# Packed attention, a mixture of experts and a soft mixture on one core: w1's loads on another queue, combine steps and a second attention group at other slots

## The chip, the core and the metric

The kernel runs on one core of a Trainium2 chip. Its engines work side by side, each through a queue of its own, strictly in order: TensorE (PE, with its weight loads PEld), VectorE (DVE), ScalarE (ACT), GpSimd (POOL) and SyncE (SP, which here only issues DMAs). The metric is the device time of one execution in microseconds, the median of a few runs.

## What is computed

```
p_packed = softmax(p k^T / 8) v          # 4 batches, 8 heads, 576 tokens, 32 packed tokens, d 64
x = softmax(q p_packed^T / 8) p_packed   # as rows: 2304 x 512
x = sum_e prob[:, e] * (relu(x @ w1[e]) @ w2[e])                  # 4 experts, F = 1024
logits = x @ phi                                                  # 32 slots
d = softmax over rows;  slots = d^T x;  per slot's expert: relu(slots @ m1) @ m2     # 8 experts
out = softmax over slots(logits) @ slot_out
```

All of it in float32. The big products are split: `a`, the second attention matrix, and `g`, the packed tokens times w1, are each held as a rounded part and a residue in float32r, and three of the four products are taken.

## The kernel before

Attention is not multiplied out. For each batch, p_packed (tile `pkn`) is multiplied with w1 first, and the result `g` then with the attention matrix `a`: that is the relu's input h. The logits come from h through `wphi`, w2 times phi, which the kernel makes once at the start.

**Slots.** The main loop runs over 128 slots, 32 a batch. A slot is one 128-wide piece of F: 12 matmuls give two banks h (L620), ScalarE takes relu (L630) and GpSimd multiplies by the expert's probability (L631); every second slot, VectorE does both for one of the banks (L625). One slot later VectorE transposes the piece into `hr` (L641, `flip_h`). Each fourth slot also makes the next `g` (`make_g`: 16 matmuls L585, two casts on ScalarE L595, two residues on VectorE L597), then loads the next half expert of w1 (`load_w1`, tile `w`, 1 MB) into its single buffer, and adds the last four pieces to the logits (`logits`, L653).

**What is hung onto slots.** A table `todo` and generators put other work behind a slot's matmuls:
- `attention` for the next batch, as two groups of heads (g = 0, 1) of 18 stages, one a slot, begun at the slots `ATT_AT` of the batch. The stages that matter here: 0 transposes of k (`kt`, L344, then q's load); 2 scores `sa` on PE; 3 row maxima (L382); 4 exponentials `ex` on ScalarE (L395); 5 normalisation on VectorE (L408 to L413); 6 transposition `et` on PE (L419); 7 copies of et and transposes of q; 8 `pv` on PE, 9 copies into `pkn` by ScalarE and VectorE (L468, L471); 10 scores `sb` on PE; 11 `nat` on VectorE (L500, L506; it frees sb's banks); 12 to 15 subtract, exponential, sum ("add", L520 to L522), multiply, by turns on GpSimd, ScalarE, VectorE, GpSimd; 16 transposition; 17 `hi`, ScalarE's cast to `a` (L537), and `lo`, its residue (L542).
- `softmaxes` of the batch before, over rows for d and over slots for the combine. The steps to d and the pooling (`POOL_AT`, L775) come first; the remaining six are the combine steps at `C_AT`: den and the row minimum on VectorE (L740, L743; from the second batch on also L735, L738), subtract on GpSimd (L745), exponential on ScalarE (L749), sum on VectorE (L751 to L753), multiply on GpSimd (L755), transposition into `cts` on VectorE (L758).
- w2's way to wphi (`wphi_ops`), for eight pieces n in the first slots: four rounds of w2t on PE and a copy back by ScalarE (L260, L267), `pw` (L275), ScalarE's copy of it (`pick`, L286), `wp` (`back`, L291), ScalarE's copy of that (`keep`, L294). Two ScalarE operations of it are let out per slot.

PE's results go through eight PSUM banks of which six rotate, the one idle longest first (`mm_ps`). A DMA that is issued waits, besides for its buffer, for the earlier DMA that uses the same one of eight completion semaphores.

**The order** of the program is written by hand (`manual_schedule`), except that the work of the head, before slot 0, is placed by `place_ops` with costs; what it leaves over (rank 2) runs in the slots in the order of its list. All loads go through SP's queue, dprobs' excepted.

**The tail**, after slot 127, streams 42 MB of w2, m1 and m2 in 512 KB chunks through whatever buffers are free, and computes the slots' experts and the output from it. The stream begins in the last batch.

Of the kernel before, what the change touches and what calls it, by code (L numbers as in the profile page):

```python
# [9 lines left out]
F32 = mybir.dt.float32  # L10
F32R = mybir.dt.float32r
AF = mybir.ActivationFunctionType
ALU = mybir.AluOpType
# [5 lines left out]
def tile_packed_attention_moe_softmoe(  # L19
# [21 lines left out]
    NB, H, S, D = q.shape  # L41
# [7 lines left out]
    NCH = NE * DF // FC  # L49
# [7 lines left out]
    HT_BUFS = 5  # L57
    W2_BUFS = 4
    POOL_AT = (5, 6, 7)
    ATT_AT = (8, 12)  # L60
    C_AT = (8, 9, 10, 11, 12, 13)
    SPREAD_AT = (2, 3)
    RING = NE + 1

# [103 lines left out]
    def load_w1(t=None):  # L168
        n = w1_n[0]
        if n >= NB * NCH:  # L170
            return
        w1_n[0] += 1
        e, hf = order[n // 2], n % 2
        if t is None:
            t = w1_pool.tile([128, NDC, FC], F32, tag="w1", name=f"w1_{n}")
        sp.dma_start(
            t, w1[e, :, FC * hf : FC * hf + FC].rearrange("(c p) f -> p c f", p=128)
        )
        w1_t[n] = t
# [18 lines left out]


    class Op:  # L200
        def __init__(self, stage, eng, cost, fn, deps, take=0, give=0, rank=0):
            self.stage, self.eng, self.cost, self.fn = stage, eng, cost, fn
            self.deps, self.take, self.give, self.rank = list(deps), take, give, rank
            self.end = None
# [41 lines left out]
        )  # L246
        w2_t[n] = t

    def wphi_ops(n, loaded, next_load):

        st = {}
        ops = []
# [1 line left out]
        def turn(x):  # L254
            t = st.setdefault("t", None)
            if t is None:
                t = st["t"] = w2_t.pop(n)
            st[x] = mm_ps(f"w2t{n}_{x}", keep=True)
            for dc in range(NDC):
                pe.transpose(  # L260
                    st[x][:, 128 * dc : 128 * dc + 128],
                    t[:, x, 128 * dc : 128 * dc + 128],
                    ident,
                )

        def put(x):
            act.copy(st["t"][:, x, :], st[x])  # L267
            let_go([st[x]])
# [24 lines left out]
        def keep():  # L293
# [2 lines left out]
            )  # L296
            let_go([st["ps"]])

        puts = []
        for x in range(4):  # L300
            ops.append(Op(0, "PE", 0.47, lambda x=x: turn(x), [loaded], take=1, rank=2))
            ops.append(Op(0, "ACT", 0.58, lambda x=x: put(x), [ops[-1]], give=1, rank=2))
            puts.append(ops[-1])
        ops.append(Op(0, "PE", 1.3, project, puts, take=1, rank=2))
        if next_load:
            next_load.deps.append(ops[-1])
            ops.append(next_load)
        pr = [o for o in ops if o.fn is project]
        ops.append(Op(0, "ACT", 0.27, pick, pr, give=1, rank=2))
        ops.append(Op(0, "PE", 0.15, back, ops[-1:], take=1, rank=2))  # L310
        ops.append(Op(0, "ACT", 0.27, keep, ops[-1:], give=1, rank=2))
        return ops


# [11 lines left out]
    def attention(b, g, tmp, late, gp, loads=None):  # L326
# [212 lines left out]
        @op(17, "DVE", 0.76, hi)  # L539
        def lo():  # L540
            hl = a2_t[b, g]
            (dve if loads else gp).tensor_tensor(out=hl[1], in0=st["a2"], in1=hl[0].bitcast(F32), op=ALU.subtract)  # L542

        return ops

# [336 lines left out]
    with tc.manual_schedule():  # L882
# [89 lines left out]
        for n in range(NCH):  # L972
            after = None
            if n + W2_BUFS < NCH:
                m = n + W2_BUFS
                after = Op(
                    0, "SP", 2.5, lambda m=m: load_w2(m, w2s[m % W2_BUFS]), [], rank=2
                )
                landed.append(after)
            ops += wphi_ops(n, landed[n], after)  # L980
            ops.append(Op(0, "NONE", 0.0, done, ops[-1:], rank=2))
        rest = place_ops(ops)
        for o in list(rest):
            if o.eng == "ACT" and all(d.end is not None for d in o.deps):
                o.fn()
# [328 lines left out]
```

## Time and profile before

| | |
|---|---|
| median of 3 runs | 508.59 us (506.87 to 512.04) |
| the profiled execution | 507.49 us, its span 505.7 us |
| PE busy | 472.3 us, 93% of the span |
| DVE, POOL, ACT busy | 290.9, 204.4, 181.7 us |
| granted TensorE clock, mean | 0.976 |
| moved by DMA | 104.36 MB |

Span is from the first instruction's start to the last one's end. PE's share of busy time says little about one place; what PE waits for, and for how long, is read from the list of waits and from the order of time. In the rows, "<-X" behind idle time names what ended it. Idle time of PEld that PE does not share costs nothing.

### The profile page before, as it was taken

To read this page: it belongs to the slowest core of one execution; us is meant where nothing else is said; L and a number is where in the kernel's file an instruction comes from. 1 tells how busy PE (TensorE), PEld (TensorE's weight loads), DVE (VectorE), ACT (ScalarE), POOL (GpSimd) and SP (SyncE) were. 2 spreads that over 40 slices of the span, in tenths; PEclk is the share of its full clock that TensorE was granted. 3 is DMA by queue.
4 is the path that set the end of the run, shared out by engine and by line. 5 is a ranking of instruction groups with operands and counts; after the bars stand their busy time and mean duration, and the time that the engine had idled before them with its cause. 6 is when DMAs were issued, how large, how long until landed. Compare 5 with 4: busy or idle time off the path is not lost.

```text
span 505.7 us, 13249 instructions
## 1 busy us (share of the span) xinstructions
PE 472.3 (93%) x5608; PEld 334.9 (66%) x5608; DVE 290.9 (58%) x551; ACT 181.7 (36%) x449; POOL 204.4 (40%) x266
## 2 busy tenths in 40 slices
PE   6899799999999989999998999999999998998695
PEld 3767677778775767778566678775787866322153
DVE  3683355687781777886559588781875545100022
ACT  2475455435440434354224335440434310200033
POOL 3024233357942544586326157941656513100000
PEclk9999999999999999999999899999999997899986
DMA  8989832457231447643215243285672479999997
GB/s 197 382 311 272 298 130 81 135 136 232 84 123 47 131 141 178 177 143 112 86 68 194 71 128 103 86 294 207 244 256 85 166 275 403 414 412 412 383 383 273
DMA packets 57740, 104.36 MB, mean 206 GB/s; under 512 B 5904, under 2 KB 24848, under 8 KB 57680
## 3 DMA queue, kind: packets, MB, share of 16 engines
q1 hardware_dynamic: 57552, 103.36, 59.6%
q8 instruction: 44, 0.72, 0.6%
q0 software_dynamic: 128, 0.15, 0.3%
q14 instruction: 16, 0.13, 0.1%
HBM read 98.78 MB, written 4.72 MB: 205 GB/s over the span
## 4 chain that ended last, share of the span: by engine, by line
PE 77%; DMA 12%; DVE 6%; SPq 3%; ACT 1%; issue 1%; ACTq 0%; DVEq 0%
PE h L620 39%; PE pb L775 8%; PE lg L653 7%; PE g L585 6%; DMA ck<-in_moe_w_dram 4%; DMA hr<-in_moe_w_dram 4%; DMA w<-in_moe_w_dram 4%; PE pv L455 3%; PE sa L358 2%; PE o L1273 2%; SPq L849 2%; PE w2t L260 2%; PE sb L358 2%; PE et L419 1%; PE tt L1133 1%; PE so L1242 1%
## 5 line engine op out<-in xcount | busy, mean ns | idle before, releaser
L631 POOL TENSOR_TENSOR ht<-ht,pe 128x288 f32<-128x288 f32 x192 | 153.1, 807 | 180.0 <-ACT ht L630 179.8
L620 PEld LDWEIGHTS h<-a,g 128*128 128x128 f32 x1536 | 207.2, 188 | 23.2 <-issue 14.7
L620 PE MATMUL h<-a,g 128*128 128x288 f32 x1536 | 222.1, 300 | 0.0
L630 ACT ACTIVATE ht<-h 128x288 f32<-128x288 f32 x192 | 79.0, 412 | 173.6 <-PE h L620 166.3
L641 DVE STREAM_TRANSPOSE hr<-ht 128x576 f32<-128x576 f32 x128 | 97.3, 763 | 45.3 <-POOL ht L631 41.9
L597 DVE TENSOR_TENSOR g<-g,g 128x512 fp32r<-128x512 f32 x64 | 40.9, 679 | 26.2 <-ACT g L595 26.2
L625 DVE SCALAR_TENSOR_TENSOR ht<-h,pe 128x288 f32<-128x288 f32 x64 | 28.0, 438 | 37.5 <-PE h L620 37.5
L595 ACT CAST g<-g 128x512 fp32r<-128x512 f32 x64 | 34.5, 589 | 27.4 <-PE g L585 27.4
L775 PE MATMUL pb<-hr,d 32*32 32x512 f32 x1152 | 40.5, 598 | 0.0
L585 PE MATMUL g<-w,pkn 64*32 64x512 f32 x512 | 36.1, 601 | 2.9 <-DMA w<-in_moe_w_dram 2.8
L653 PE MATMUL lg<-ht,wphi 128*32 128x288 f32 x512 | 38.3, 412 | 0.0
L653 PEld LDWEIGHTS lg<-ht,wphi 128*32 128x32 f32 x512 | 13.5, 109 | 33.2 <-POOL ht L631 22.5
L775 PEld LDWEIGHTS pb<-hr,d 32*32 32x32 f32 x1152 | 18.3, 103 | 14.7 <-issue 10.2
L1233 DVE COPY ob<-o 128x256 f32<-128x256 f32 x12 | 4.7, 422 | 36.5 <-PE o L1273 36.2
L1242 PE MATMUL so<-hr,hm 128*32 128x256 f32 (+1 forms) x136 | 18.0, 455 | 4.7 <-DMA hr<-in_moe_w_dram 4.7
L267 ACT COPY hr<-w2t 128x512 f32<-128x512 f32 x32 | 17.5, 595 | 5.5 <-PE w2t L260 5.4
L260 PE MATMUL w2t<-ident,hr 128*128 128x128 f32 x128 | 18.3, 290 | 0.7 <-ACT pt L286 0.6
L260 PEld LDWEIGHTS w2t<-ident,hr 128*128 128x128 f32 x128 | 15.5, 149 | 3.4 <-issue 0.9
L673 POOL COPY ps<-dpn 128x576 f32<-128x576 f32 x16 | 10.6, 665 | 13.7 <-DVE dpn L195 13.7
L789 DVE SCALAR_TENSOR_TENSOR tacc<-tacc,rsc,pb 128x512 f32<-128x512 f32 x12 | 8.2, 743 | 13.2 <-PE pb L775 13.2
L1242 PEld LDWEIGHTS so<-hr,hm 128*32 128x32 f32 x136 | 6.1, 116 | 14.1 <-DMA hr<-in_moe_w_dram 9.4
L1242 PE MATMUL so<-ck,hm 128*32 128x512 f32 (+1 forms) x52 | 12.3, 531 | 1.1 <-DMA ck<-in_moe_w_dram 1.1
(159 smaller groups left out, 435.4 us busy)
## 6 DMA issues: line engine op xcount, KB each, us to landing
w<-in_moe_w_dram SPq DMA_DIRECT2D x32, 1024.0 KB, 5.2
hr<-in_moe_w_dram SPq DMA_DIRECT2D x40, 512.0 KB, 8.7
ck<-in_moe_w_dram SPq DMA_DIRECT2D x38, 512.0 KB, 8.0
hr<-in_moe_w_dram SPq DMA_DIRECT2D x8, 1024.0 KB, 10.1
k<-in_k_dram SPq DMA_DIRECT2D x16, 288.0 KB, 3.9
v<-in_v_dram SPq DMA_DIRECT2D x18, 192.0 KB, 7.0
q<-in_q_dram SPq DMA_DIRECT2D x12, 288.0 KB, 2.9
out_dram<-ob SPq DMA_DIRECT2D x8, 384.0 KB, 6.0
```

The source lines that it names most:

```text
L260: pe.transpose(st[x][:, 128 * dc : 128 * dc + 128], t[:, x, 128 * dc : 128 * dc + 128], ident,)
L585: pe.matmul(ps[g][c : c + 32, :], pkn_t[b][o : o + 64, g, hp, 0, :], t[o : o + 64, 2 * g + hp, :], start=True, stop=True, tile_position=(o ...
L595: act.copy(gg[:, 0, g], ps[g])
L597: dve.tensor_tensor(out=gg[:, 1, g], in0=ps[g], in1=gg[:, 0, g].bitcast(F32), op=ALU.subtract)
L620: pe.matmul(ps[:, :HS], gg[:, l, g, fs], m[:, ts], start=(g == 0 and i == 0), stop=(g == 1 and i == 2),)
L625: dve.scalar_tensor_tensor(out=ht[:, ts], in0=ps[:, :HS], scalar=0.0, in1=pr[:, ts], op0=ALU.max, op1=ALU.mult,)
L630: act.activation(out=ht[:, ts], in_=ps[:, :HS], func=AF.Relu)
L631: pool.tensor_tensor(out=ht[:, ts], in0=ht[:, ts], in1=pr[:, ts], op=ALU.mult)
L641: dve.transpose(out=hr[:, place(b, i), :, f0 : f0 + 32], in_=ht_t[s].rearrange("p (x t) -> p x t", t=32),)
L653: pe.matmul(lg_t[b][r][32 * x : 32 * x + 32, :HS], wphi[:, NFT * e + 4 * hf + x, :], ht_t[4 * ci + x][:, HS * r : HS * r + HS], start=(ch ...
L775: pe.matmul(pb[c][m : m + 32, :], d[o, x + par, :], hr[o, lo : hi + 1 : hi - lo, x + par, :], start=(x == 0), stop=(x == NBLK - 2), tile_p ...
L1242: pe.matmul(so[32 * e : 32 * e + 32, d0 : d0 + dw], hm[s][:, x + xl, e, :], cks[e][:, dw * xl : dw * xl + dw], start=(s == 0 and x + xl == 0),
```

## The change

Five edits. w1's loads for n = 1 to 25 are issued by ScalarE, behind the two casts of make_g; n = 0 and those of the last batch stay with SP. The six combine steps move from slots 8 to 13 of a batch to slots 17 to 26. The second attention group begins at slot 13 of a batch in place of 12. The list of w2's way back is sorted by a key, so that `wp` and its copy of piece n come behind the second w2t of piece n + 1. The residue of `a` is always VectorE's.

```
-    ATT_AT = (8, 12)
-    C_AT = (8, 9, 10, 11, 12, 13)
+    ATT_AT = (8, 13)
+    C_AT = (17, 18, 19, 21, 22, 26)
...
-        sp.dma_start(
+
+        (act if 0 < n < (NB - 1) * NCH + 2 else sp).dma_start(
             t, w1[e, :, FC * hf : FC * hf + FC].rearrange("(c p) f -> p c f", p=128)
         )
...
+        def add(eng, cost, fn, deps, key, **kw):
+            ops.append(Op(0, eng, cost, fn, deps, rank=2, key=n + key, **kw))
+            return ops[-1]
+
         puts = []
         for x in range(4):
...
+            tr = add("PE", 0.47, lambda x=x: turn(x), [loaded], 0.1 * x, take=1)
+            puts.append(add("ACT", 0.58, lambda x=x: put(x), [tr], 0.1 * x, give=1))
+        pr = add("PE", 1.3, project, puts, 0.5, take=1)
         if next_load:
-            next_load.deps.append(ops[-1])
+            next_load.deps.append(pr)
+            next_load.key = n + 0.5
             ops.append(next_load)
...
+        pk = add("ACT", 0.27, pick, [pr], 0.5, give=1)
+
+        bk = add("PE", 0.15, back, [pk], 1.15, take=1)
+        kp = add("ACT", 0.27, keep, [bk], 1.15, give=1)
+        add("NONE", 0.0, done, [kp], 1.15)
         return ops
...
-            (dve if loads else gp).tensor_tensor(out=hl[1], in0=st["a2"], in1=hl[0].bitcast(F32), op=ALU.subtract)
+            dve.tensor_tensor(out=hl[1], in0=st["a2"], in1=hl[0].bitcast(F32), op=ALU.subtract)
...
-        rest = place_ops(ops)
+        rest = sorted(place_ops(ops), key=lambda o: o.key)
```

Three places in the order, before and after. Line numbers after are two to seven higher than before (L260 is L262, L408 is L415, L641 is L648).

TensorE in the first batch, around one pw; before:

```order
L275 MATMUL pw_786<-hr,tacc 32x128 x16
L291 MATMUL wp_805<-ident,pt_803 128x128
L620 MATMUL h_0_810<-a_00_509,g_603 128x288 x3
L620 MATMUL h_0_810<-a_01_541,g_603 128x288 x3
L620 MATMUL h_1_819<-a_00_509,g_603 128x288 x3
L620 MATMUL h_1_819<-a_01_541,g_603 128x288 x3
L260 MATMUL w2t_0_827<-ident,hr 128x128 x4
L260 MATMUL w2t_1_833<-ident,hr 128x128 x4
```

The same place after:

```order
L277 MATMUL pw_786<-hr,tacc 32x128 x16
L262 MATMUL w2t_0_805<-ident,hr 128x128 x4
L627 MATMUL h_0_813<-a_00_509,g_603 128x288 x3
L627 MATMUL h_0_813<-a_01_541,g_603 128x288 x3
L627 MATMUL h_1_822<-a_00_509,g_603 128x288 x3
L627 MATMUL h_1_822<-a_01_541,g_603 128x288 x3
L262 MATMUL w2t_1_830<-ident,hr 128x128 x4
L293 MATMUL wp_836<-ident,pt_803 128x128
```

The reader of pt, wp, has moved behind the next slot and both w2t; the number of rows is the same.

VectorE at slots 12 and 13 of the second batch (g residues, then what stands ahead of the first group's normalisation, the rows of ss and ex); before:

```order
L597 TENSOR_TENSOR g_2441<-g_0_2442,g_2441 128x512
L597 TENSOR_TENSOR g_2441<-g_1_2443,g_2441 128x512
L344 STREAM_TRANSPOSE kt_2471<-k_1494 128x576
L344 STREAM_TRANSPOSE kt_2473<-k_1496 128x576
L641 STREAM_TRANSPOSE hr<-ht_2422 128x18x32
L625 SCALAR_TENSOR_TENSOR ht_2480<-h_1_2490,pe_2013 128x288
L758 STREAM_TRANSPOSE cts<-lt_1991 32x576
L408 TENSOR_SCALAR ss_2468<-ss_2468 128x1
L412 RECIPROCAL ss_2468<-ss_2468 128x1
L413 TENSOR_SCALAR ex_2467<-ex_2467,ss_2468 128x576
```

The same place after:

```order
L604 TENSOR_TENSOR g_2433<-g_0_2434,g_2433 128x512
L604 TENSOR_TENSOR g_2433<-g_1_2435,g_2433 128x512
L648 STREAM_TRANSPOSE hr<-ht_2414 128x18x32
L632 SCALAR_TENSOR_TENSOR ht_2463<-h_1_2473,pe_2013 128x288
L415 TENSOR_SCALAR ss_2459<-ss_2459 128x1
L419 RECIPROCAL ss_2459<-ss_2459 128x1
L420 TENSOR_SCALAR ex_2458<-ex_2458,ss_2459 128x576
L351 STREAM_TRANSPOSE kt_2484<-k_1540 128x576
L351 STREAM_TRANSPOSE kt_2486<-k_1542 128x576
```

The second group's k transposes have moved behind the normalisation, and the transposition into cts has gone from here. The combine's sum (L751 to L753), which stood a slot ahead of these rows, has gone too.

VectorE ahead of the second group's copy into pkn, with the next transposition behind it, slots 20 and 21 of the second batch; before:

```order
L641 STREAM_TRANSPOSE hr<-ht_2778 128x18x32
L625 SCALAR_TENSOR_TENSOR ht_2853<-h_1_2863,pe_2412 128x288
L471 COPY pkn_2323<-pv_2823 32x2x32 x2
L641 STREAM_TRANSPOSE hr<-ht_2853 128x18x32
L520 TENSOR_REDUCE bm_2764<-nat_2761 128x18
L521 TENSOR_SCALAR bm_2764<-bm_2764 128x18
L522 RECIPROCAL bm_2764<-bm_2764 128x18
```

After, slots 21 and 22:

```order
L648 STREAM_TRANSPOSE hr<-ht_2762 128x18x32
L632 SCALAR_TENSOR_TENSOR ht_2819<-h_1_2829,pe_2407 128x288
L758 TENSOR_REDUCE cm_2671<-lt_1991 128x18
L759 TENSOR_SCALAR cm_2671<-cm_2671 128x18
L760 RECIPROCAL cm_2671<-cm_2671 128x18
L648 STREAM_TRANSPOSE hr<-ht_2819 128x18x32
L527 TENSOR_REDUCE bm_2751<-nat_2748 128x18
L528 TENSOR_SCALAR bm_2751<-bm_2751 128x18
L529 RECIPROCAL bm_2751<-bm_2751 128x18
L478 COPY pkn_2320<-pv_2841 32x2x32 x2
```

The sum of the combine and the first group's add now stand ahead of the copy.

## Rows read from the trace of the kernel before

**Rows 1.** The page's busy times and two groups of its part 5 (busy, mean ns).

```profile
PE 472.3 (93%) x5608; PEld 334.9 (66%) x5608; DVE 290.9 (58%) x551; ACT 181.7 (36%) x449; POOL 204.4 (40%) x266
...
L620 PE MATMUL h<-a,g 128*128 128x288 f32 x1536 | 222.1, 300 | 0.0
...
L641 DVE STREAM_TRANSPOSE hr<-ht 128x576 f32<-128x576 f32 x128 | 97.3, 763 | 45.3 <-POOL ht L631 41.9
```

**Rows 2.** Busy time by stretch: us, PE, PEld, DVE, ACT, POOL, clock, DMA share, GB/s.

```profile
440.00:456.00 16.00, 15.54 (x140) 5.36 (x139) 3.05 (x16) 0.60 (x1) 0.00 (x0) 1.00 1.02 413
```

**Rows 3.** PE's waits: line waited for, total us, times, longest.

```profile
PE et L419 <- DVE ex L413: 4.7, 2, 2.5
PE g L585 <- DMA w<-in_moe_w_dram: 2.8, 2, 2.5
PE wp L291 <- ACT pt L286: 2.5, 5, 0.8
```

**Rows 4.** PE in order of time: start, us, operation, idle before in brackets.

```profile
40.52 1.09 PE L585 MATMUL g<-w,pkn 64*32 64x512 f32 x16 [0.32 <-DMA w<-in_moe_w_dram]
...
45.67 0.33 PE L291 MATMUL wp<-ident,pt 128*128 128x128 f32 x1 [0.75 <-ACT pt L286]
...
54.97 1.09 PE L585 MATMUL g<-w,pkn 64*32 64x512 f32 x16 [2.46 <-DMA w<-in_moe_w_dram]
...
58.48 0.33 PE L291 MATMUL wp<-ident,pt 128*128 128x128 f32 x1 [0.44 <-ACT pt L286]
```

**Rows 5.** Loads: an issue, w1's issues, landing (page), queue, two stretches.

```profile
46.34 0.40 SPq L176 DMA_DIRECT2D w<-in_moe_w_dram  x1
...
L176 SPq DMA_DIRECT2D w<-in_moe_w_dram x32: 367/379/1718, 14.9 to 383.5; - x32
...
w<-in_moe_w_dram SPq DMA_DIRECT2D x32, 1024.0 KB, 5.2
...
q1 hardware_dynamic: 57552, 103.36, 59.6%
...
30.00:32.50 2.50, 1.92 (x32) 1.48 (x20) 2.24 (x6) 2.36 (x6) 1.13 (x1) 1.00 0.41 45
33.00:40.00 7.00, 6.93 (x101) 5.90 (x101) 4.45 (x8) 5.70 (x15) 1.16 (x1) 1.00 1.03 385
```

**Rows 6.** VectorE, ScalarE and PE in order of time, batch 2, slots 9 to 14.

```profile
169.87 0.75 DVE L743 TENSOR_REDUCE cm<-lt 128x18 f32<-128x576 f32 x1
...
176.43 0.71 DVE L751 TENSOR_REDUCE cm<-lt 128x18 f32<-128x576 f32 x1
...
177.75 0.75 DVE L382 TENSOR_REDUCE mx<-sa 128x1 f32<-128x288 f32 x2
...
179.90 0.22 ACT L395 ACTIVATION_READ_ACCUMULATOR ex<-sa,mx 128x1 f32 x1
...
180.53 1.42 DVE L344 STREAM_TRANSPOSE kt<-k 128x576 f32<-128x576 f32 x2
...
184.62 0.83 PE L419 MATMUL et<-ident,ex 128*96 128x128 f32 x6 [2.20 <-DVE ex L413]
```

**Rows 7.** Busy time by stretch, behind the wait in batch 3.

```profile
279.60:283.00 3.40, 3.40 (x38) 2.03 (x39) 0.34 (x1) 0.00 (x0) 0.00 (x0) 0.50 0.00 0
```

**Rows 8.** VectorE's nat and PE's g at slots 19 and 20 of batch 2.

```profile
201.62 0.81 DVE L500 STREAM_TRANSPOSE nat<-sb 128x288 f32<-128x288 f32 x2
...
202.16 1.49 PE L585 MATMUL g<-w,pkn 64*32 64x512 f32 x16
```

**Rows 9.** Busy time from 200.50 to the pkn copy, and the second sb.

```profile
200.50:209.40 8.90, 8.88 (x117) 6.86 (x115) 7.73 (x16) 4.00 (x11) 4.12 (x5) 1.00 0.44 120
...
209.59 0.71 PE L358 MATMUL sb<-qt,pkn 32*32 32x288 f32 x16
```

**Rows 10.** The residue of a: instructions, min/median/max ns, first and last start.

```profile
L542 POOL TENSOR_TENSOR a<-a2t,a x6: 1433/1440/1447, 125.1 to 323.1; 128x576 fp32r<-128x576 f32 x6
L542 DVE TENSOR_TENSOR a<-hr,a x2: 758/758/759, 35.5 to 37.8; 128x576 fp32r<-128x576 f32 x2
```

## What the change does to the time, predicted blind

> **What bounds the kernel now.** I read the page's busy times first: PE (TensorE) works through 93% of the span [rows 1], so the time is the sum of what PE is given plus the places where it stands still, and an engine that is merely busy costs nothing. A slot of the main loop, one 128-wide piece of F, takes PE 222.1/128 = 1.74 us [rows 1]. From 405 us on, the combine's weights are streamed; there the DMA engines are full (share 1.02, 413 GB/s) [rows 2]. That stream goes into buffers which the main loop frees at its end, so I count a microsecond won before 405 us as won at the end, and expect nothing else of the last 100 us: the change leaves the last batch's loads on SP's queue, and the chunks' order too. Then I listed what PE itself waits for, leaving out waits of engines that nobody waits for. Three entries stand in stages that the change touches: et for VectorE's normalised ex (4.7 us, 2 times), g for a w1 load (2.8 us, 2 times), wp for ScalarE's copy of pw (2.5 us, 5 times) [rows 3]. The forecast is about these three, and about what the moved work makes late instead.
>
> **1. w2's way back.** Before, pw is followed at once by wp, which reads ScalarE's copy of pw: PE waits 0.75 us at 45.67 and 0.44 us at 58.48, and three more times like the second [rows 4]. After, w2t_0 of the next piece stands behind pw and a whole slot (1.74 us) lies before wp, longer than any of these waits. The matmuls and copies are the same ones. The last of the five has no next piece and keeps its 0.44. Won: 0.75 + 3 x 0.44 = 2.07 us. w2t_0 now needs its w2 piece a slot earlier; those loads were issued one to three pieces ahead, so I put nothing for it. Were that cover gone, the wait returns at w2t_0, at most the 2.07.
>
> **2. w1 on ScalarE's queue.** Before, the load w_2 stands in SP's queue behind p's four, k's four and v's three loads of batch 1 and is issued at 46.34 [rows 5]; g(2) waits for it 2.46 us at 54.97 [rows 4]. After, it is issued right behind ScalarE's casts of g(1), some 3 us earlier, and in a queue of its own. Bounds: nothing won (it still shares the engines with k, v and two w2 pieces) and 2.46. I take 2.46, since the head start alone is longer than the wait.
> The price is at w_1. It is now issued only behind a ScalarE copy, while before it followed a w2 piece directly on SP's queue, and it competes with the next w2 piece for 385 GB/s [rows 5]. PE already waits 0.32 us for it at 40.52 [rows 4]. Bounds for the added wait: 0 (DMA was nearly idle from 30.0 to 32.5, 45 GB/s [rows 5], so some of a later start is there to be used) and one whole 1 MB load at that rate, 1.05 MB / 385 GB/s = 2.7 us. I take 0.5, nearer the lower end, because only the w2 piece issued after it competes.
> An issue also costs ScalarE time: 0.38 us by the median of the same DMA on SP [rows 5]. There are 25 of them; ScalarE is 36% busy [rows 1], so behind a g they lie in its idle time. Only w_2's issue has something urgent behind it: the copy of w2t_3 that pw needs. It waits, too, for one of p's loads, with which it shares a completion semaphore. I put 0.3 for it, from 0 to 1. Part 2: +2.46 - 0.8.
> A rule of the Trainium skill speaks against this part ("DMA: Bandwidth & Descriptors", Issuing engines are not separate DMA queues): transfers started by several engines run on the same 16 DMA engines and interleave, so that a second issuer saves only issue time. By it w_2 could keep its wait and the sum would be 2.46 smaller. The trace has all its hardware DMAs on one queue [rows 5], so no row here decides it; it is the second rival.
>
> **3. Combine steps later, second group one slot later.** In batches 2 and 3 the first et waits 2.20 us (184.62) [rows 6] and the rest of the 4.7 us, 2.47, for the normalisation on VectorE. ScalarE had the exponentials done at 179.90 + 0.22 = 180.12 [rows 6], 3.5 us before VectorE got to it. Ahead of it in VectorE's queue stood: the combine's sum (176.43 to 177.75, 1.32 us), the second group's two k transposes (1.42 us) [rows 6], and the transposition into cts. The order after has all three gone from there. PE arrives at 184.62 - 2.20 = 182.42. What is left ahead of the norm (one transpose, one multiply) and the norm itself fit in the 2.3 us from 180.12, barely; bounds 0 and 0.5 of remaining wait, I take 0.2.
> The 2.47 us in batch 3 was followed by 3.40 us at the half clock, 0.50 of 2.4 GHz [rows 7]; PE does half its work there, so 1.7 us are lost. The 2.20 us in batch 2 was followed by nothing of the kind. With the wait gone I count the 1.7 as won; bounds 0 and 1.7.
> A third wait goes: g at 202.16 takes 1.49 us against 1.09 for the same 16 matmuls at 54.97 [rows 4, 8]. It takes the banks of sb, which VectorE's nat frees at 201.62 + 0.81 = 202.43 [rows 8]. After, et stands between, a slot later, so nat is done first: 0.40 in each of three batches.
> **What becomes late instead** is VectorE in slots 17 to 23 of a batch, where combine steps and attention now meet. At slot 17 the row minimum (0.75 us, 169.87 [rows 6]) and the den step stand ahead of the copy into pkn that sb reads: bounds 0 and 0.9, I take 0.3. Second place: the second group's copy into pkn, with sb one slot later. Before, from 200.50 on VectorE had 7.73 us of work [rows 9] up to that copy, and sb began at 209.59, 9.1 us later. After, its queue holds 7.73 + 1.32 (the sum) + 1.32 (the add, three instructions like it, now ahead of the copy) + 0.76 (a transpose of one more slot [rows 1]) = 11.1 us; PE gives it 9.1 + 1.74 (one more slot) + 0.7 (et now inside) - 0.4 = 11.1 us. So it is full. On top, VectorE stands still before the residue of g, since et's copy and the q transposes now come behind it. I put 0.8, between 0 and the 1.8 us that those take. New waits: 0.2 + 0.3 + 0.8 = 1.3 us in batches 2 and 3, none in batch 1, which has no combine steps.
>
> **4. The residue of a on VectorE**: 0.758 us there instead of 1.44 us on GpSimd [rows 10], six times. GpSimd was not on the path; VectorE is, in part 3's stretch, but these six lie behind it. The second group's stands two slots before its reader, so between it and the next batch's first matmuls lies one slot, 1.74 us, for a relu and a cast on ScalarE and the 0.758 us. I put 0, with 0.3 in each batch as the upper bound, both estimates.
>
> **Sum.** Head: 2.07 + 2.46 - 0.8 = 3.7. Batch 1: 0.4. Batch 2: 2.20 + 0.40 - 1.3 = 1.3. Batch 3: 2.47 + 1.7 + 0.40 - 1.3 = 3.3. Together 8.7 us. The profiled execution took 507.49 us, its span 505.7 and 1.8 around it; 507.49 - 8.7 = 498.8. The runs shown have their median 1.1 us above it (508.59), so as a median of runs I forecast 499.9 us.
>
> **Rivals.**
> - *VectorE gives it back.* If the stretch of part 3 runs slower than its rows, the wait moves from et to sb, and in batches 2 and 3 as much is lost as is won, clock included. Left: 3.7 + 0.4 = 4.1, so 504.5. For it: that stretch was full by my own count. Against: VectorE has 1.3 us idle in the 9.1 us before. Chance 0.17.
> - *The loads interleave*. w_1 gets half of 385 GB/s beside the w2 piece and lands 2 us later, and w_2 beside k, v and w2 keeps g(2) waiting: 8.7 - 1.4 - 2.46 = 4.8, so 503.8. For it: DMA is full from 33 to 40 us [rows 5]. Against: small loads that are queued ahead no longer hold w_2 back. Chance 0.12. The rule of the Trainium skill in part 2 is what would bring this about.
> - *The norm waits for something else* and et's 4.7 us and the clock stay: 8.7 - 4.67 - 1.7 + 0.4 = 2.7, so 505.9. Against: ex was done 3.5 us earlier. Chance 0.05.
> - *Slower: ScalarE is held by its own DMA issues.* An issue waits for an earlier transfer on the same semaphore; if that one is just under way, ScalarE stands still up to a landing, 5.2 us [rows 5], its relus free no banks and PE stops. It decides from 0.6 us of PE per issue: 25 x 0.6 = 15 us eat the 8.7 and 6 more, 514.9. Against: outside the head, the transfers before it on each semaphore were issued several slots earlier. Chance 0.05.
>
> **How the numbers follow.** Main case 0.60 (own range 496.5 to 503: all new waits zero give 12 us, the upper bounds of parts 2 and 3 take 3 us more), then 0.17, 0.12, 0.05, 0.05, and 0.01 for the rest. About 1% is what a measurement of this kernel can tell from no change; 1% under 508.59 is 503.5. Faster: 0.60 and about half of the second and a third of the first rival, 0.72. Slower 0.06, same 0.22. The range from 496 to 505 leaves out the two rare rivals and a tail of the others.
>
> **What would show it.** Right: the wait of et for ex under 1 us in all, g for w under 1 us, wp at one wait of 0.44, no half clock near 280 us, w's DMAs on ScalarE. New: waits of sb for VectorE's or ScalarE's pkn, up to 1 us each, in batches 2 and 3 alone. Wrong: sb waits of 2 us and more; g(1) waiting over 1 us for w_1; ScalarE idle behind a DMA issue; or h at a batch's first slot waiting for the residue of a.

## The result, and the profile after

The changed kernel took 502.15 us in the median of 4 runs (500.04 to 504.38) beside 508.43 us before, a ratio of 0.9858 with a 95% interval of 0.9814 to 0.9902. Timed again beside the experiments below, it gave 0.9809 (0.9775 to 0.9844). So the two measurements put it 1.4 and 1.9% below the kernel before. The forecast was 499.9 us, with a range of 496.0 to 505.0. The total lies in the range, but not all of its terms were right: what moved in the attention and the combine steps won about what was forecast, w1's other queue won nothing that shows in the main loop, and the end of a batch lost 0.8 us where no loss was forecast.

The profiled execution took 502.67 us with a span of 500.9, that is 4.8 us less than before on either count; 8.7 had been forecast on that basis. The start of each g cuts the main loop into like pieces, g(0) being the first one made. Times in us, the forecast by the terms of the sum:

| stretch | before | after | change | forecast |
|---|---|---|---|---|
| up to g(0) | 26.93 | 27.37 | +0.44 | 0 |
| head: g(0) to g(5) | 69.35 | 68.20 | -1.15 | -3.7 |
| batch 1: g(5) to g(11) | 70.54 | 71.06 | +0.52 | -0.4 |
| batch 2: g(11) to g(19) | 93.61 | 92.43 | -1.18 | -1.3 |
| batch 3: g(19) to g(27) | 95.72 | 92.70 | -3.02 | -3.3 |
| g(27) to the last logits | 51.39 | 51.37 | 0.0 | 0 |
| the rest | 98.2 | 97.8 | -0.4 | 0 |

The page's busy times and queues of the kernel after; 25 loads of w1 now run through a queue of their own (q10):

```profile
PE 473.1 (94%) x5608; PEld 335.2 (67%) x5608; DVE 295.4 (59%) x557; ACT 181.7 (36%) x449; POOL 198.6 (40%) x260
...
q1 hardware_dynamic: 44352, 77.15, 44.5%
q10 hardware_dynamic: 13200, 26.22, 15.8%
```

What PE waits for after (line waited for, total us, times, longest), against [rows 3]:

```profile
PE pw L277 <- ACT hr L269: 1.9, 1, 1.9
...
PE h L627 <- DVE a L549: 0.6, 3, 0.2
PE g L592 <- ACT ht L637: 0.5, 1, 0.5
PE wp L293 <- ACT pt L288: 0.4, 1, 0.4
PE g L592 <- DMA w<-in_moe_w_dram: 0.4, 1, 0.4
```

The wait of et for ex is gone, wp's is down from 2.5 to the one 0.4 that was to stay, g's wait for w from 2.8 to 0.4 (that is g(0)'s; the 0.5 under ScalarE's name is g(2)'s and belongs to w too, see below). New are pw's 1.9 us and h's 0.6.

**The head after**, in order of time (start, us, engine, operation, idle before in brackets; ACTq is ScalarE's queue of DMA issues):

```profile
44.45 0.37 ACTq L177 DMA_DIRECT2D w<-in_moe_w_dram  x1
45.17 0.27 ACT L296 COPY wphi<-wp 128x128 f32<-128x128 f32 x1 [2.63 <-DMA k<-in_k_dram]
45.33 0.59 ACT L269 COPY hr<-w2t 128x512 f32<-128x512 f32 x1
...
45.98 1.14 PE L277 MATMUL pw<-hr,tacc 128*32 128x128 f32 x26 [1.94 <-ACT hr L269]
...
55.81 1.09 PE L592 MATMUL g<-w,pkn 64*32 64x512 f32 x16 [0.46 <-ACT ht L637]
```

ScalarE's casts of g(1) ended at 42.54, and its next operation ran at 45.17. Between them stood the issue of w_2, which went out at 44.45. It shares a completion semaphore with p's second load for batch 1, and that landed at 44.38 (the profile puts the wait down to a load of k). The copy of w2t behind it was what pw needed. In the stretch behind pw's wait the granted clock fell, to half from 48 to 50 us (us, PE, PEld, DVE, ACT, POOL, clock, DMA share, GB/s):

```profile
45.98:50.60 4.62, 4.62 (x43) 4.34 (x44) 0.78 (x1) 1.52 (x4) 1.27 (x2) 0.63 1.04 273
50.60:55.81 5.21, 4.75 (x40) 4.55 (x38) 2.58 (x4) 3.48 (x8) 3.24 (x5) 1.00 1.08 275
```

And w_2, though issued 1.9 us earlier than before, landed at 55.67 in place of 54.83: the DMA engines were full all that time. The 0.46 us of g(2) stand under ScalarE's name in the list, but it is this landing, 0.14 us ahead of the start, that came last.

**Batch 2 after**, in order of time: VectorE's norm, PE's et, the g behind the second sa, and the first sb, against [rows 6]:

```profile
181.48 0.52 DVE L420 TENSOR_SCALAR ex<-ex,ss 128x576 f32<-128x576 f32 x1
...
182.15 0.83 PE L426 MATMUL et<-ident,ex 128*96 128x128 f32 x6
...
187.42 1.09 PE L592 MATMUL g<-w,pkn 64*32 64x512 f32 x16
...
194.46 1.53 PE L365 MATMUL sb<-qt,pkn 32*32 32x288 f32 x32
```

The norm ends at 182.00, 0.15 us ahead of et, which no longer waits; sb, whose reads come a little late now, takes 0.34 us longer than before:

```profile
196.93 1.20 PE L358 MATMUL sb<-qt,pkn 32*32 32x288 f32 x32
```

In batch 3 the clock is whole around the place of the old wait (columns as above; the half clock of [rows 7] stood there):

```profile
268.00:288.00 20.00, 20.00 (x252) 14.91 (x256) 16.48 (x35) 9.59 (x27) 8.24 (x12) 1.00 0.55 163
```

**The end of batch 1 after**, where before there was no stall:

```profile
128.69 2.32 POOL L638 TENSOR_TENSOR ht<-ht,pe 128x288 f32<-128x288 f32 x3
...
129.21 1.49 PE L660 MATMUL lg<-ht,wphi 128*32 128x288 f32 x16
...
130.63 5.56 PE L627 MATMUL h<-a,g 128*128 128x288 f32 x40
...
135.60 0.76 DVE L549 TENSOR_TENSOR a<-a2t,a 128x576 fp32r<-128x576 f32 x1
...
136.41 1.33 PE L627 MATMUL h<-a,g 128*128 128x288 f32 x8 [0.22 <-DVE a L549]
```

The same place before:

```profile
130.20 1.18 PE L653 MATMUL lg<-ht,wphi 128*32 128x288 f32 x16
131.31 6.64 PE L620 MATMUL h<-a,g 128*128 128x288 f32 x48
```

The same 16 matmuls lg took 1.18 us before, and now 1.49, since GpSimd is late with the products that they read. At 136.41 h, in the first slot of the next batch, waits for the residue of a; the 48 matmuls h of that quarter take 0.48 us longer than before. The quarter from g(8) to g(9) takes 9.49 us in place of 8.70, and so it does in batches 2 and 3.

### The profile page after: what moved, and what is told of

It is laid out like the page before. It is cut to its first block, busy times and chain, and to the rows that moved or that the text cites. A ratio compares the mean times of both kernels' runs of the same rounds, so it can differ in the third digit from the quotient of the medians.

```text
span 500.9 us, 13284 instructions
## 1 busy us (share of the span) xinstructions
PE 473.1 (94%) x5608; PEld 335.2 (67%) x5608; DVE 295.4 (59%) x557; ACT 181.7 (36%) x449; POOL 198.6 (40%) x260
## 4 chain that ended last, share of the span: by engine, by line
PE 67%; DMA 16%; DVE 8%; ACT 2%; SPq 2%; POOL 2%; issue 1%; POOLq 0%; DVEq 0%; ACTq 0%
PE h L627 35%; PE pb L782 8%; PE lg L660 6%; PE g L592 6%; DMA ck<-in_moe_w_dram 5%; DMA w<-in_moe_w_dram 4%; DMA hr<-in_moe_w_dram 4%; PE pv L462 2%; DMA k<-in_k_dram 2%; SPq L856 2%; PE w2t L262 2%; PE sb L365 2%; DMA hr<-in_v_dram 2%; DVE hr L648 2%; DVE g L604 1%; PE sa L365 1%
## 5 line engine op out<-in xcount | busy, mean ns | idle before, releaser
L627 PE MATMUL h<-a,g 128*128 128x288 f32 x1536 | 225.6, 301 | 0.6 <-DVE a L549 0.6
L627 PEld LDWEIGHTS h<-a,g 128*128 128x128 f32 x1536 | 207.8, 189 | 26.8 <-issue 14.7
L638 POOL TENSOR_TENSOR ht<-ht,pe 128x288 f32<-128x288 f32 x192 | 154.9, 816 | 178.4 <-ACT ht L637 178.0
L648 DVE STREAM_TRANSPOSE hr<-ht 128x576 f32<-128x576 f32 x128 | 97.6, 763 | 41.6 <-POOL ht L638 38.8
L592 PE MATMUL g<-w,pkn 64*32 64x512 f32 x512 | 34.9, 601 | 0.9 <-ACT ht L637 0.5
L262 PE MATMUL w2t<-ident,hr 128*128 128x128 f32 x128 | 19.2, 292 | 0.3 <-ACT hr L269 0.2
L262 PEld LDWEIGHTS w2t<-ident,hr 128*128 128x128 f32 x128 | 15.4, 150 | 3.8 <-issue 1.3
L680 POOL COPY ps<-dpn 128x576 f32<-128x576 f32 x16 | 10.8, 678 | 14.3 <-DVE dpn L196 14.3
```

Source lines behind the costliest of these rows:

```text
L262: pe.transpose(st[x][:, 128 * dc : 128 * dc + 128], t[:, x, 128 * dc : 128 * dc + 128], ident,)
L592: pe.matmul(ps[g][c : c + 32, :], pkn_t[b][o : o + 64, g, hp, 0, :], t[o : o + 64, 2 * g + hp, :], start=True, stop=True, tile_position=(o ...
L627: pe.matmul(ps[:, :HS], gg[:, l, g, fs], m[:, ts], start=(g == 0 and i == 0), stop=(g == 1 and i == 2),)
L638: pool.tensor_tensor(out=ht[:, ts], in0=ht[:, ts], in1=pr[:, ts], op=ALU.mult)
L648: dve.transpose(out=hr[:, place(b, i), :, f0 : f0 + 32], in_=ht_t[s].rearrange("p (x t) -> p x t", t=32),)
```

## The experiments

Lengths of the pieces that tell the kernels apart, in us. The last column counts the three pieces of batches 2 and 3 in which et, sb and nat lie. Between g(2) and g(26) a piece repeats within 0.1 us from one execution to the next where nothing was edited in it; ahead of g(2) it does not.

| kernel | g(1) to g(2) | w_2 issued, landed | g(8) to g(9) | g(12) to g(15) / g(20) to g(23) |
|---|---|---|---|---|
| before | 14.45 | 46.34, 54.83 | 8.70 | 37.25 / 39.13 |
| after | 15.50 | 44.45, 55.67 | 9.49 | 35.28 / 35.55 |
| after, again | 12.89 | 44.81, 53.76 | 9.46 | 35.28 / 35.52 |
| att12 | 13.01 | 42.98, 51.27 | 8.70 | 37.00 / 37.25 |
| lo_pool | 14.68 | 43.41, 54.28 | 10.22 | 35.29 / 35.53 |
| c_old | 14.28 | 43.59, 53.98 | 9.47 | 35.83 / 36.56 |
| spread12 | 13.75 | 44.96, 54.83 | 10.61 | 35.41 / 35.90 |
| no_key | 13.33 | 43.59, 50.61 | 9.48 | 35.29 / 35.54 |
| w1_sp (two executions) | 13.78, 13.35 | 45.10, 52.96 and 45.83, 53.48 | 9.47 | 35.30 / 35.54 |
| defer | 12.68 | 45.16, 52.63 | 9.46 | 35.29 / 35.55 |
| pkv_late | 11.11 | 41.80, 48.65 | 9.46 | 35.27 / 35.55 |
| best | 11.08 | 40.71, 48.94 | 9.36 | 35.28 / 35.54 |
| best_sp | 11.11 | 41.45, 46.94 | 9.35 | 35.28 / 35.55 |

Where no total time is given, the verdict comes from these pieces.

### The attention and the combine steps

**att12**: the second group back at slot 12.

```diff
-    ATT_AT = (8, 13)
+    ATT_AT = (8, 12)
```

> The changed kernel with the second attention group back at slot 12. Read from the start times of g, which in the changed kernel are 128.19 and 137.68 in batch 1 (9.49 us apart, 0.79 more than the 8.70 before), and 199.95. Theory 'one slot too late': the 0.79 us in each of batches 1 to 3 come from the second group's add and multiply, which at slots 27 and 28 meet the copies and the transposition of the next probabilities and the residue of g. Then the 0.79 goes in all three batches (-2.4 us), and the stall of g behind sb and nat comes back with 0.40 each (+1.2 us, less what the extra changes of work cost, 0.2 each), so the main loop ends 1.2 to 1.8 us earlier. Rival 'residue on VectorE': the 0.79 stays, because it is VectorE's residue of a that is late. For the et wait: with the k transposes (1.42 us) back ahead of the norm, et waits again for what is left, 2.20 less the sum and cts' transposition (1.32 and 0.76), 0.1 to 0.4 us, in batches 2 and 3.

The 0.79 us went in all three batches (8.70), and g's stall came back: g(14) to g(15) grew by 0.19, g(6) to g(7) by 0.21. But et waits far more than the 0.1 to 0.4 us expected in each of batches 2 and 3:

```profile
PE et L426 <- DVE ex L420: 3.5, 4, 1.0
```

Against the changed kernel batches 2 and 3 lose 1.72 and 1.70 us in the last column's pieces and win 0.79 each at their ends, and batch 1 wins 0.5: the later slot is worth 1.3 us net, not a loss. "One slot too late" is right about the 0.79 and wrong about the sum.

**c_old**: the combine steps back at slots 8 to 13, the second group staying at 13.

```diff
-    C_AT = (17, 18, 19, 21, 22, 26)
+    C_AT = (8, 9, 10, 11, 12, 13)
```

> The changed kernel with the combine steps back at slots 8 to 13, the second group staying at slot 13. By the prediction's part 3 the norm stood behind the sum (1.32 us), the k transposes (1.42) and cts' transposition (0.76). Only the k transposes are gone here, so the first et of batches 2 and 3 should wait 2.20 - 1.42 = 0.8 and 2.47 - 1.42 = 1.0 us, and sb's new waits of 0.34 and 0.24 us in batch 2 (0.59 in batch 3) should go, since no combine step stands in slots 17 to 23. Net against the changed kernel: +1.8 - 1.2 = +0.6 us, and up to 1.7 more if the half clock comes back in batch 3. Rival: moving either part alone is enough to free the norm, so et waits nothing and the kernel is 1.2 us faster at the end of the main loop than the changed one.

```profile
PE et L426 <- DVE ex L420: 2.8, 2, 1.8
```

et waits 1.04 us in batch 2 and 1.8 in batch 3, expected were 0.8 and 1.0; sb's waits went. Most of the surplus in batch 3 is one instruction, the norm's multiply on VectorE: it takes 1.15 us here beside GpSimd's multiplies, and 0.52 in the changed kernel, with GpSimd idle.

```profile
274.24 1.15 DVE L420 TENSOR_SCALAR ex<-ex,ss 128x576 f32<-128x576 f32 x1
```

Net, batch 2 lost 0.55 us and batch 3 1.25, where 0.6 had been expected of the two together. The table holds both edits, each done and undone, with the other three edits in place. In batch 2 the second group's slot alone wins 1.42 us of the 37.25 (c_old; et's wait is 1.16 us shorter than before there), the combine steps alone win 0.25 (att12), both 1.97. In batch 3 it is 2.57, 1.88 and 3.58; the half clock stayed away in all three. Neither alone frees the norm.

**lo_pool**: the residue of a on GpSimd again.

```diff
-            dve.tensor_tensor(out=hl[1], in0=st["a2"], in1=hl[0].bitcast(F32), op=ALU.subtract)
+            (dve if loads else gp).tensor_tensor(out=hl[1], in0=st["a2"], in1=hl[0].bitcast(F32), op=ALU.subtract)
```

> The changed kernel with the residue of a back on GpSimd (1.44 us) for the six late instances. Theory 'one slot too late': the 0.79 us of batches 1 to 3 stays or grows by a few tenths, since GpSimd is part of what is crowded there. Rival 'residue on VectorE': the 0.79 us goes in all three batches, 2.4 us earlier at the end of the main loop. The prediction had put the residue at nothing: then the main loop ends within 0.3 us of the changed kernel's.

Order of time at the batch's end (as above), where h now waits for GpSimd:

```profile
135.79 1.32 PE L627 MATMUL h<-a,g 128*128 128x288 f32 x8 [0.90 <-POOL a L549]
```

The quarter takes 10.22 us, 0.73 more than with VectorE's residue, in each of three batches. So the residue on VectorE is not what makes the stall; it takes 2.2 us out of it in the three batches. Part 4 of the prediction had it at nothing.

**spread12**: the next probabilities a slot earlier.

```diff
-    SPREAD_AT = (2, 3)
+    SPREAD_AT = (1, 2)
```

> The changed kernel with the spreading of the next expert's probabilities (GpSimd's copy ps 0.66 us, VectorE's transposition pe 0.76 us) one slot earlier, at slots 1 and 2 of each eight in place of 2 and 3. Theory 'one slot too late': the crowd at slots 26 to 28 is the second group's add and multiply beside ps, pe and the residue of g. With pe and ps a slot earlier the 0.79 us of each batch shrinks to 0 to 0.4, the main loop ends 1.2 to 2.4 us earlier. Rival 'residue on VectorE': no change, 0.79 stays. A new stall may come at slots 17 and 18, where pe then meets the first group's copies: up to 0.4 us a batch.

Both theories missed: the quarter grew to 10.61. PE's waits name the engine:

```profile
PE lg L660 <- POOL ht L638: 2.4, 3, 0.8
```

A slot earlier, GpSimd's copy of the probabilities (0.66 us) falls beside the second group's subtraction (1.16), and the products that lg reads come later still. GpSimd's queue is the crowded one for lg, VectorE's for h. The new stall at slots 17 and 18 that had been thought possible came: 0.13 and 0.35 us in the last column's pieces.

### The head

Two theories stood here. "Landing": w_2 lands when the bytes ahead of it are through, whoever issues it. "Hold": what is lost is ScalarE's stand at the issue.

**defer**: the issue of w_2 alone moved behind slot 1's work on ScalarE.

```diff
         let_go(ps)
-        load_w1()
+        if ci != 1:
+            load_w1()
...
+            if s == 1:
+                load_w1()
```

> The changed kernel with the issue of w_2 alone moved behind slot 1's work on ScalarE, so that it finds its completion semaphore free and holds nobody up. Theory 'landing': pw no longer waits, but w_2, issued 1 to 2 us later into full DMA engines, lands at 55.7 to 57.5, and the whole saving turns up as a wait of g(2) for w (2.5 to 5 us); g(2) starts 15.4 to 17 us behind g(1). Rival 'hold': the 1.94 us and the half clock behind it are lost on the path, so without them g(2) starts 12 to 13.5 us behind g(1), about 3 us earlier than in the changed kernel.

No wait of pw, and g(2) 12.68 us behind g(1), as "hold" had it. But g(2) then waits for the load, as "landing" had it, though less:

```profile
43.40 1.08 PE L277 MATMUL pw<-hr,tacc 128*32 128x128 f32 x32
45.16 0.42 ACTq L177 DMA_DIRECT2D w<-in_moe_w_dram  x1
...
52.77 1.09 PE L592 MATMUL g<-w,pkn 64*32 64x512 f32 x16 [1.52 <-DMA w<-in_moe_w_dram]
```

Neither theory alone holds: both costs are there, and the later one shows.

**w1_sp**: all of w1's loads on SP's queue.

```diff
-        (act if 0 < n < (NB - 1) * NCH + 2 else sp).dma_start(
+        sp.dma_start(
```

> The changed kernel with all of w1's loads on SP's queue. In the changed kernel g(1) starts at 40.31 and g(2) at 55.81, 15.50 us later: pw stands 1.94 us because ScalarE is held by the issue of w_2 from 42.54 to 44.45, the clock is at about half for some 3 us behind it, and w_2 lands at 55.67. Theory 'landing': from 33 to 61 us the DMA engines are full, w_2 lands when the bytes queued ahead are through, whoever issues it; g(2) starts right behind it. Then w_2 lands at 54.8 as before the change, g(2) starts 14.3 to 14.7 us behind g(1), with a wait for w of about 3 us in place of ScalarE's hold, and the head is about 0.9 us faster than in the changed kernel. Theory of the prediction 'queue': w_2 on ScalarE wins 2.46 - 0.8 us; then g(2) comes 1.7 us later than in the changed kernel.

```profile
45.10 0.40 SPq L177 DMA_DIRECT2D w<-in_moe_w_dram  x1
...
53.09 1.09 PE L592 MATMUL g<-w,pkn 64*32 64x512 f32 x16 [2.63 <-DMA w<-in_moe_w_dram]
```

g(2) waits 2.63 us for the load, and still stands 13.78 us behind g(1), earlier than "landing" (14.3 to 14.7) and "queue" (17.2) had it, and within the changed head's own scatter: that head ran in six executions (after, after again, att12, lo_pool, c_old, spread12) and took 12.89 to 15.50, 14.0 in the mean. From its issue w_2 took between 8.3 and 11.2 us to land in them. In four of the six (after, lo_pool, c_old, spread12) g(2) starts 0.13 or 0.14 us behind w_2's landing; in the other two w_2 is there 0.4 and 1.0 us earlier, and pw's wait counts. So the edit mostly moved a wait from one place to another: g(2) itself waits 0 to 1.65 us for w in the six, beside 2.2 to 2.6 with w_2 on SP's queue, and pw waits 1.4 to 1.9 us that it did not wait before. The first profile, with its 15.50, was the worst of the six, and the only one in which the clock fell behind pw's wait.

**no_key**: w2's way back in the old order.

```diff
-        rest = sorted(place_ops(ops), key=lambda o: o.key)
+        rest = place_ops(ops)
```

> The changed kernel with w2's way back in its old order, wp right behind pw. The prediction's part 1 counted 0.75 + 3 x 0.44 = 2.07 us for the new order. Theory 'landing': what is won ahead of g(2) is lost again in waiting for w_2, so here g(2) starts at the same time behind g(1) as in the changed kernel (15.5 us, within 0.3), though wp waits 0.75 there, and only the waits behind g(2), 3 x 0.44 = 1.3 us, come on top. Rival: the full 2.07 us come on top, 0.75 of it between g(1) and g(2).

```profile
46.59 0.33 PE L293 MATMUL wp<-ident,pt 128*128 128x128 f32 x1 [0.41 <-ACT pt L288]
...
56.89 0.33 PE L293 MATMUL wp<-ident,pt 128*128 128x128 f32 x1 [0.44 <-ACT pt L288]
```

Behind g(2) the old order costs 0.69 and 0.81 us in the two pieces to g(4), 1.5 in all (expected 1.3): this part of the edit is worth its term. The 15.5 us up to g(2) did not repeat (13.33), and w_2 landed 2.8 us ahead of g(2); whether the wait ahead of g(2) counts can't be read out of that scatter.

**pkv_late**: the loads of batch 1's p, k and v, needed from slot 8 on, moved from ahead of slot 0 to slot 3.

```diff
-        load_p(1)
-        for g in range(2):
-            load_two(k, "k", 1, g)
-        load_v(1, 0)
...
+            if s == 3:
+                load_p(1)
+                for g in range(2):
+                    load_two(k, "k", 1, g)
+                load_v(1, 0)
```

> The changed kernel with the loads of the next batch's p, k and v (2.3 MB, needed from slot 8 on) issued at slot 3, behind w_2 and the last two w2 pieces, instead of ahead of slot 0. Theory 'landing': w_2 waits for bytes; with 2.3 MB fewer ahead of it it lands before 50 us and g(2) starts at 12 to 12.8 us behind g(1) in place of 15.5, no wait of pw, no half clock; the main loop ends about 3 us earlier. Theory 'queue' of the prediction: w_2's own queue already lets it pass p, k and v, so only ScalarE's hold goes (its semaphore is then another one): 1.9 us, and a wait of g(2) for w of about 1 us stays. Danger for both: sa of the first group at slot 10 waits for k if the loads land after 75 us.

```profile
40.58 1.09 PE L592 MATMUL g<-w,pkn 64*32 64x512 f32 x16 [0.96 <-DMA w<-in_moe_w_dram]
...
41.80 0.38 ACTq L177 DMA_DIRECT2D w<-in_moe_w_dram  x1
43.89 1.08 PE L277 MATMUL pw<-hr,tacc 128*32 128x128 f32 x32
...
51.69 1.09 PE L592 MATMUL g<-w,pkn 64*32 64x512 f32 x16
```

w_2 goes out between ScalarE's two casts, another transfer being on its semaphore now, and lands at 48.65, 3 us before g(2) asks for it: 11.11 us, and no wait of g(2) or pw. That is 1.8 to 4.4 us better than the changed head's six. The price is none that shows: sa of the next batch does not wait, and the pieces up to g(26) are the same. The one from g(26) to g(27) takes 20.11 us, 0.8 more than in the changed kernel, but it scatters (19.27 to 20.11 in all the traces), and no_key, where these loads are not moved, has 19.96.

### Timed together

**best** takes pkv_late, puts w_1 back on SP's queue, and the spreading of a batch's first probabilities one slot later; **w1_sp_timed** is w1_sp again, **after_again** the changed kernel itself.

```diff
-                at(8 * (n - 1) + i, lambda spread=spread: next(spread))
+                at(8 * (n - 1) + i + (n % 4 == 0), lambda spread=spread: next(spread))
...
-        (act if 0 < n < (NB - 1) * NCH + 2 else sp).dma_start(
+        (act if 1 < n < (NB - 1) * NCH + 2 else sp).dma_start(
```

> The changed kernel with p's, k's and v's loads for batch 1 at slot 3, w_1 on SP's queue again (w_2 to w_25 stay on ScalarE's), and the spreading of the next batch's first probabilities one slot later (GpSimd's ps at slot 27, VectorE's pe at slot 28, where they stand at 26 and 27 in the changed kernel). From the runs so far: one slot earlier made lg wait for GpSimd and took the quarter from 9.49 to 10.61 us, so one slot later should take ps from ahead of the products that lg reads and pe from ahead of the second group's add: lg's 0.31 goes, and the residue of a, which h waits for, comes up to 0.76 earlier, so that the 9.49 us of batches 1 to 3 become 8.7 to 9.0 (-1.5 to -2.4 us). Rival: pe at slot 28 falls among the residues of g and delays the next h; then 9.5 us and more stay. Head: g(2) 11 to 11.3 us behind g(1), as in the run with p, k and v at slot 3 alone, and a wait of g(1) of 0.3 in place of 0.96. Together the main loop ends 4 to 6 us earlier than in the changed kernel, near 397 to 399 us, and the time is 495 to 498 us, 0.975 to 0.982 of the kernel before; if only the head helps, 498 to 500.

> The changed kernel with all of w1's loads on SP's queue, timed. In single looks of the changed head g(2) came 13.0 to 15.5 us behind g(1), mean 14.2 over five executions with the same head, against 13.8 here. Theory 'landing': the queue doesn't matter, the time stands within 1 us of the changed kernel's in the same runs (ratio of the two within 0.998 and 1.002, unclear which is faster). Theory 'queue' of the prediction: 1.7 us slower than the changed kernel, 0.3 per cent.

> The changed kernel itself beside the other two, as their base on the same chip: 0.9858 of the kernel before so far (0.9814 to 0.9902), so 501 to 502 us. Its head tells how much the landing of w_2 varies: g(2) 13.0 to 15.5 us behind g(1); the rest of the main loop, from g(2) on, repeats to 0.1 us a segment.

| kernel | median (range), us | ratio to before (95% interval) |
|---|---|---|
| best | 498.55 (497.99 to 500.19) | 0.9779 (0.9743 to 0.9816) |
| w1_sp_timed | 502.09 (500.11 to 502.68) | 0.9832 (0.9795 to 0.9869) |
| after_again | 500.25 (499.92 to 501.23) | 0.9809 (0.9775 to 0.9844) |

best's head repeats at 11.08 us, and its main loop ends at 398.08 in place of 401.32 (after_again). The time lies where it was put for the case that only the head helps. The spreading hardly helped: lg's 0.31 went, but h waits longer for the residue, which VectorE now reaches later, and the quarter is 9.36.

```profile
131.03 1.32 PE L627 MATMUL h<-a,g 128*128 128x288 f32 x8 [0.40 <-DVE a L549]
```

best is 1.7 us below the changed kernel timed beside it, though their intervals overlap. w1_sp_timed is 1.8 us above it, as "queue" had it (1.7), and their intervals overlap too; its main loop ends at 400.98, 0.3 us earlier than after_again's.

**best_sp**: best with every load of w1 on SP's queue, so that nothing of the queue edit is left.

> The previous best version (p, k and v of batch 1 at slot 3, the next batch's first probabilities a slot later) with all of w1's loads back on SP's queue, so that nothing of the queue edit is left. Theory 'bytes ahead': what the head needed was only that w_2 doesn't stand behind p, k and v, and SP's queue serves as well as ScalarE's; then w_2 is issued before 42 and lands before 50, g(2) starts 11 to 11.3 us behind g(1) without a wait, every later segment is as in that version, and the ratio to the kernel before is within its interval, 0.974 to 0.982. Theory 'queue': in SP's queue w_2 or a later load of w1 stands behind a w2 piece that waits for TensorE; then g(2) or g(3) waits 1 us or more for w, and the ratio is 0.004 or so higher, as the 1.8 us between the two timed medians of the changed kernel with and without the queue edit (500.25 and 502.09) would have it.

```profile
41.45 0.37 SPq L177 DMA_DIRECT2D w<-in_moe_w_dram  x1
...
51.35 1.09 PE L592 MATMUL g<-w,pkn 64*32 64x512 f32 x16
```

w_2 lands at 46.94, g(2) comes 11.11 us behind g(1), and every piece from g(1) to g(26) is best's within 0.1 us. "Bytes ahead" is shown for the main loop: what w_2 needed was not to stand behind p, k and v. The time was 499.53 us (498.20 to 501.22), a ratio of 0.9829 (0.9783 to 0.9874), 0.005 above best's, as "queue" had it for the total (0.004); the intervals overlap. Twice the version with SP's queue alone came out 0.2 to 0.5% slower, each time within the uncertainty. Of the 2.5 us of span between the profiles of best and best_sp 0.9 stand at 470 us, and 1.6 arise in the next 5 us, where the same 26 matmuls `so` run at a clock of 1.00 in best (first line) and 0.53 in best_sp (second line):

```profile
470.52 1.91 PE L1249 MATMUL so<-hr,hm 128*32 128x256 f32 x26 [0.74 <-DMA hr<-in_moe_w_dram]
471.38 3.54 PE L1249 MATMUL so<-hr,hm 128*32 128x256 f32 x26 [0.74 <-DMA hr<-in_moe_w_dram]
```

In the mean from there to the end the clock is 0.70 in best_sp, 0.81 in best, 0.96 in after_again, 0.83 in w1_sp_timed, 0.72 in att12, so it goes with neither queue in these few profiles. Whether the queue itself is worth a microsecond at the end stays open.

## Why the prediction came out as it did

**The frame held.** PE is the bound, and what is won ahead of 405 us comes out at the end, but for the scatter of the last stretch: from the last logits on the profiles take 97.6 to 101.4 us, 98.2 before, the longer ones at a lower clock in the last 26 us where this was read. In all fourteen traces the last load of the stream lands 83.6 to 84.5 us behind the last logits; the scatter arises behind it, where 13.9 to 16.9 us are left.

**Part 3 was right in its main terms.** The norm came in time (no wait of et), and behind it the half clock of batch 3 stayed away: g(20) to g(21) fell by 4.16 us, forecast 2.47 + 1.7 = 4.17. g's stall behind nat went, but won 0.2 instead of 0.40; that PE now changes between kinds of work more often may be the reason, but no run shows it. The new waits were together smaller than forecast: sb's 0.34 and 0.24 us in batch 2 for 0.3 and 0.8, et's none for 0.2. That the sums of batches 2 and 3 came out all the same was luck: a stall that I hadn't placed there, 0.79 us at the batch's end, made up for the waits that stayed small.

**Part 4 was wrong in size.** I put 0 for the residue of a, with 0.3 as the upper bound, because a slot lay between it and its reader. That slot still lies there in the order, but the chain came too late to use it: VectorE reached the transposition ahead of it 5.9 us behind g(8), at 134.10, where it had been 3.0 us before the change, and the later slot is only 1.74 us of that. The residue ran from 135.60 to 136.36, and h, four matmuls into the next batch, stood until then. h takes 0.48 us longer, lg, held up by GpSimd, 0.31: 0.79 in each of three batches, batch 1 included, where I had said that nothing new would come. With the residue on GpSimd it would have been 1.5 (lo_pool). The step that failed was to count the chain's end by slots and not by what stands ahead of it on VectorE and GpSimd there: the second group's add, the copy and transposition of the probabilities, the residues of g. That the later slot brings the 0.79 is shown (att12); which of these pieces costs how much of h's part is read from the order alone. h waiting for the residue was one of the prediction's own signs of being wrong.

**Part 1 was right behind g(2)**: 1.55 us won there, 3 x 0.44 = 1.32 forecast, and the last wp kept its 0.44. The 0.75 ahead of g(2) drowned in part 2.

**Part 2 was wrong.** Between g(0) and g(2) I forecast -0.75 - 2.46 + 0.8 = -2.4 us. The first profile showed +0.4, and the mean of the six changed heads -0.7, against a kernel before whose head was profiled once (28.0 us). The comparison with nothing else changed is w1_sp: 26.8 and 26.7 us with all of w1 on SP's queue, 27.3 in the mean of the six. The edit by itself won nothing here that stands out of the scatter. Two terms failed. First, the hold of ScalarE at w_2's issue: I named its cause, and sized it 0.3 within 0 to 1. It was 1.34 to 1.94 in seven executions, because the semaphore's earlier transfer, p's second load, was still under way in full DMA engines: in each of the seven w_2 went out 0.07 or 0.08 us behind that load's landing. ScalarE idle behind a DMA issue was another sign of being wrong that came. Second, the head start: I took 3 us and a queue of its own to mean an earlier landing. The start was 1.9 us, and the landing, measured from g(1), came 10.6 to 15.4 us behind it (mean 13.2 over seven) against 13.2 to 14.3 on SP's queue (three). So the second rival, to which I gave 0.12, was nearly the case: for w_2 by its own mechanism, the landing, with part of g(2)'s wait now standing at pw; for w_1 its price was small: g(1) waited 0 to 1.5 us, 0.5 in the mean of nine executions with w_1 on ScalarE's queue, beside 0.32 before. This is the rule of the Trainium skill that the prediction weighed ("DMA: Bandwidth & Descriptors", Issuing engines are not separate DMA queues): transfers from several engines interleave on the same DMA engines. The trace agrees with it: w_2 was issued 1.9 us earlier and landed 0.84 later. The same page of the Trainium skill says in its section "Anatomy of one DMA — SWDGE (gpsimd) path", which describes GpSimd's path, that the DMA engines wait on no semaphore and any such wait is spent by the issuing engine's sequencer ahead of dispatch; the trace agrees for ScalarE, which stood 1.9 us ahead of the issue.

**The other rivals.** VectorE did not give back the win, the norm waited for nothing else, and outside the head ScalarE was not held: from g(4) to g(26) no piece grew but where the attention and the batch's end lie.

## What to carry to other kernels

A load that was late in full DMA engines was helped here by taking away what was queued ahead of it and wasn't needed yet, not by another queue; and an engine that computes should issue only DMAs whose completion semaphore is surely free, since its whole queue stands behind the issue. When a chain is moved by a slot, look at its last link too: name its reader, and what its engines have queued in that slot. And before a term of a busy head is trusted to a microsecond, see how far that head scatters from one execution to the next.

## What was not expected of the hardware

The same load of 1 MB in the same head took 8.3 to 11.2 us from issue to landing in six executions, beside 5.2 in the median of all w1 loads [rows 5], and the piece around it 12.89 to 15.50 us, while the attention's pieces repeat to 0.1 us. The norm's multiply on VectorE (`ex<-ex,ss`), the same instruction each time, took 0.52 us in all 24 cases of the fourteen traces in which GpSimd ran nothing beside it, and 0.53 to 1.15 in the 60 in which GpSimd did; what couples the two was not tested. And a stall of 1.94 us in the head was followed by a stretch at 0.63 of the full clock, those of 1.34 to 1.55 us by none (clock 1.00 from 44 to 50 us), as before the change 2.47 us at 278.74 was followed by the half clock [rows 7] and 2.20 us at 184.62 by none.
